# Sums of a head's values in spare columns of the weighted sums' bank

## The chip, the cores and the metric

The kernel runs on one core of a Trainium2 chip. The metric is the time of one execution on the device in microseconds (us); the median of several runs is compared. A core has five engines with a queue of instructions each, which they work off in order: TensorE (PE: matmuls, their weights are loaded by PEld), VectorE (DVE), ScalarE (ACT), GpSimd (POOL) and SyncE (SP, which here issues the DMAs). TensorE writes its results into PSUM, which has eight banks of 512 fp32 columns in each of 128 partitions; VectorE and ScalarE read them there.

## The reference

The program is an attention over clusters followed by two feed-forward layers. 2 batches x 8 heads, 768 tokens, 64 columns a head, 16 centroids a head:

```python
q_assign = argmax(q_n @ c_n.T)           # each query's cluster, k_assign likewise for keys
mask = q_assign[:, :, :, None] == k_assign[:, :, None, :]
scores = where(mask, (q @ k.T) / 8, -1e9)
attn = exp(scores - max(scores)); attn = attn / (sum(attn) + 1e-9)
x = attn @ v                             # heads joined: 1536 x 512
h = x @ moe_w_in;  x = softplus(h) @ moe_w_out
h = x @ moe2_w_in; out = leaky_relu(h, 0.01) @ moe2_w_out
```

A query whose cluster holds no key gets all scores equal, so its result is the mean of all values of the head: for this the sums of a head's values over its 768 keys are needed.

## The kernel before, in words

Fp32 operands are split in two fp16 (or bf16) parts, and a product is built of the products of the parts. The 16 heads run one after another in a software pipeline, with C = 6 tiles of 128 tokens each. For a head h:

- `split` (L288) splits q and k and transposes them by DMA into "t"; `assign_mm` (L300) multiplies them by the centroids: 24 narrow matmuls (L306) into the PSUM bank "as". `assign_el` (L314) makes a one-hot row of each token's cluster in five VectorE steps (L319 to L325), of which the last reads "as". ScalarE writes the one-hot rows behind the 64 columns of q and k ("nq"), and a DMA transposes the whole into "tq" (L331).
- `emit_s1` (L340): masked scores with queries in the partitions (L345), of which VectorE takes maxima "mm" (L352). `emit_m` (L354) brings the maxima into the transposed q ("dg", L359, L361, matmuls L366, copies L374), and marks queries whose cluster is empty.
- `emit_s2` (L377), for a key tile kt of six: scores with keys in the partitions, less the maximum (L392, L393, 384 columns each), exp on ScalarE into "p" (L399), and what bf16 loses of p on GpSimd into "pl" (L401). In heads 0 to 7 the tile kt = 1 goes without "pl": its product is made of fp32.
- `emit_pv` (L406): the weighted sums of the values, six row tiles into the bank "x", 65 columns each (64 and the sum of the weights): L428, L429 and, for pl, L433; in fp32 L415. They take 390 of the 512 columns.
- `emit_sv` (L435): the sums of the head's values, twelve matmuls by a tile of ones (L439, L440) over 65 columns. They are split into a copy "h" (ScalarE, L444) and "svr" (VectorE, L445), both on partitions 96 to 127.
- `emit_empty` (L448): six small matmuls (L451) add these sums to the rows of "x" whose cluster is empty. `emit_norm` (L460) divides (L470, L471, L473) out of "x"; L470 puts six columns behind the 390 to use.

There is one bank "as" and one bank "x" (`PSUM_BUFS`, and the pool px): a new user waits until the last readers of the old one are done. In the program's order "as" is taken by the assignment of head h + 2, then by the sums of head h, then by the assignment of head h + 3. The order of each engine's queue is made when the program is built: a list scheduler takes what it expects to be ready first, by priorities (`at_pri`: the weighted sums of tile j of head h have h + j / 6, the first scores h - 4, the assignment h - 2). The waits between engines are put in where two instructions touch the same tile; for a PSUM tile the whole bank counts.

From head 8 on the first feed-forward layer of the first batch fills TensorE's gaps (`moe_steps`), from head 0 on the weights are read in and split in between (`w_step`, "wcp"). When the attention ends, TensorE runs the feed-forward layers.

Of the kernel before, what the change touches and what calls it, by code (L numbers as in the profile page):

```python
# [43 lines left out]

FF_PRI, FF_STEP, FF_RATE = 8, 0.25, 0.75

W_FREE, W_FROM, W_TO, W_PER = 4, 8, 10, 5
W_PRI = ((0, 0.5), (17, 0.3))
W2_STEPS = 88
# [7 lines left out]
def attn_moe_kernel(  # L57
# [13 lines left out]
    V, S, G, PE = nc.vector, nc.scalar, nc.gpsimd, nc.tensor  # L71
    B, H, SEQ, D = q.shape
    NCL = cen.shape[1]
    DM, DFF = w_in1.shape
    C = SEQ // 128
# [22 lines left out]
    def atile(shape, dt, tag, h):  # L98
        late, early = BUFS[tag]
        n = turn[tag] = turn.get(tag, -1) + 1  # L100
        if h < H and early and n % (late + early) >= late:
            return ep.tile(shape, dt, tag=tag, name=tag, bufs=early)
        return at.tile(shape, dt, tag=tag, name=tag, bufs=late)
# [18 lines left out]
    ones = acon.tile([128, 128], F16, name="ones")  # L122
# [4 lines left out]
    def ring(tag, h=NH):  # L127
        if h < H and tag == "s2":
            n = turn["ps" + tag] = turn.get("ps" + tag, -1) + 1
            if n % (PSUM_BUFS[tag] + 1) == PSUM_BUFS[tag]:  # L130
                return pm.tile([128, 512], F32, tag="m1", name="m")
        return pr.tile([128, 512], F32, tag=tag, name=tag, bufs=PSUM_BUFS[tag])

    mark, tki = {}, {}
    ld_t, tp1, tp2, tpq, p_t, xn_t, as_t, x_t, v_t, svs = ({} for _ in range(10))
# [141 lines left out]
    def load_v(h):  # L277
        b, hh = divmod(h, H)
        vv = v32s[h % V_BUFS][:, :, 0:D]
        nc.sync.dma_start(out=vv, in_=v[b, hh].rearrange("(p c) d -> p c d", c=C))  # L280
        v_t[h] = vv

    def split_v(h):
        vv, v2 = v_t.pop(h), v2s[h % V_BUFS]
        S.copy(out=v2[:, :, D:2 * D], in_=vv)
        ENG[by_group(VLO, h)].tensor_tensor(out=v2[:, :, 0:D], in0=vv, in1=v2[:, :, D:2 * D], op=ALU.subtract)
# [67 lines left out]
    def emit_m(h):  # L354

        dg = dgs[h % len(dgs)]
        diag = dg.rearrange("p (c s) -> p c s", s=129)
        m = diag[:, :, MR:MR + 1]
        mark[h] = V.reduce_max(out=m, in_=mms[h % 2], axis=AX)  # L359
        empty = diag[:, :, MR + C:MR + 3 * C].rearrange("p c (t s) -> p c t s", s=C)[:, :, :, 0]  # L360
        V.tensor_scalar(out=empty, in0=m.to_broadcast([128, C, 2]), scalar1=-65504.0, scalar2=None, op0=ALU.is_equal)  # L361
        t = tp2[h][0]
        for j in range(2):
            bank = ring("s2", h)
            for c in range(3 * j, 3 * j + 3):
                PE.matmul(  # L366
                    out=bank[0:KS2, (c % 3) * 128:(c % 3 + 1) * 128],
                    lhsT=dg[:, c * 128:(c + 1) * 128],
                    rhs=ident,
                    start=True,  # L370
                    stop=True,
                )
            o = bank[MR:KS2, 0:3 * 128].rearrange("p (c r) -> p c r", c=3)
            S.copy(out=t[MR:KS2, 3 * j:3 * j + 3, :], in_=o)  # L374
        tpq[h] = t
# [28 lines left out]
    XW = D + 1  # L404

    def emit_pv(h, kt):  # L406
        v2 = v2s[h % V_BUFS]
        if kt == 0:
            x_t[h] = px.tile([128, 512], F32, tag="x", name="x")
        xps = x_t[h]  # L410
        p, pb, pl = p_t.pop((h, kt))
        if pl is None:
            pf = p.rearrange("p a r -> p (a r)")
            for c in range(C):
                PE.matmul(  # L415
                    out=xps[:, c * XW:(c + 1) * XW],
                    lhsT=pf[:, c * 128:(c + 1) * 128],
                    rhs=v32s[h % V_BUFS][:, kt, :],
                    start=(kt == 0 and c == 0),
                    stop=False,  # L420
                )
            return
        pb = pb.rearrange("p a r -> p (a r)")
        pl = pl.rearrange("p a r -> p (a r)")
        for c in range(C):
            cs = slice(c * 128, (c + 1) * 128)
            o = xps[:, c * XW:(c + 1) * XW]
            PE.matmul(out=o, lhsT=pb[:, cs], rhs=v2[:, kt, D:2 * D + 1], start=(kt == 0 and c == 0), stop=False)  # L428
            PE.matmul(out=o[:, 0:D], lhsT=pb[:, cs], rhs=v2[:, kt, 0:D], start=False, stop=False)  # L429
        for c in range(C):  # L430
            cs = slice(c * 128, (c + 1) * 128)
            o = xps[:, c * XW:(c + 1) * XW]
            PE.matmul(out=o, lhsT=pl[:, cs], rhs=v2[:, kt, D:2 * D + 1], start=False, stop=False)  # L433

    def emit_sv(h):  # L435
        v2 = v2s[h % V_BUFS]
        o = ring("as")[:, 0:XW]
        for kt in range(C):
            PE.matmul(out=o, lhsT=ones, rhs=v2[:, kt, D:2 * D + 1], start=(kt == 0), stop=False)  # L439
            PE.matmul(out=o[:, 0:D], lhsT=ones, rhs=v2[:, kt, 0:D], start=False, stop=(kt == C - 1))  # L440
        q4 = slice(MR, 128)
        h16 = atile([128, XW], F16, "h16", h)
        r = atile([128, XW], F16, "svr", h)
        S.copy(out=h16[q4], in_=o[q4])  # L444
        V.scalar_tensor_tensor(out=r[q4], in0=h16[q4], scalar=sel[q4], in1=o[q4], op0=ALU.mult, op1=ALU.add)  # L445
        svs[h] = r
# [6 lines left out]
    def emit_out(b, hh, xn):  # L453
        nc.sync.dma_start_transpose(
            out=xt[b][:, hh // 2].rearrange("p n (c r) -> p (n c) r", c=C), in_=xn.rearrange("p n c d -> p (n c d)")
        )
# [34 lines left out]
    def open_late():  # L491
        actx.close()
        gp = lctx.enter_context(tc.tile_pool(name="gp", bufs=1))
        late["mt"] = lctx.enter_context(tc.tile_pool(name="mt", bufs=2))
        late["h"] = gp.tile([128, KFF, TB], F16, name="g_h")
        late["l"] = gp.tile([128, KFF, TB], F16, name="g_l")
# [228 lines left out]
    def behind_tk(h):  # L725
        return tc.issue_after(tki[h].ins) if h in tki else nullcontext()

    @contextmanager
    def at_pri(x):
        old = tc.cur_priority  # L730
        tc.cur_priority = pri(x)
        yield
        tc.cur_priority = old
# [8 lines left out]
    with at_pri(-9):  # L742
# [6 lines left out]
            out=ss[:, 1:2], in0=ss[:, 0:1], scalar1=ss[:, 2:3], scalar2=ss[:, 1:2], op0=ALU.mult, op1=ALU.add  # L749
# [19 lines left out]
    for v2 in v2s:  # L769
# [3 lines left out]
        out=ident, in_=ones, pattern=[[1, 128]], compare_op=ALU.is_equal, fill=0.0, base=0, channel_multiplier=-1  # L773
# [4 lines left out]
    for j in range(NCL):  # L778
# [4 lines left out]
        out=sel, in_=sel, pattern=[[0, 1]], compare_op=ALU.is_ge, fill=0.0, base=-MR - 2 * C, channel_multiplier=1  # L783
# [112 lines left out]
    def chain(h):  # L896
        if h < NH:
            with at_pri(h - LEAD_SPLIT):
                split(h)
            with at_pri(h - LEAD_ASSIGN):  # L900
                assign_mm(h)
                assign_el(h)
            with at_pri(h - LEAD_MAX):
                for c in range(C):
                    emit_s1(h, c)
            if h + 2 < NH:
                with at_pri(h - LEAD_LOAD):
                    load(h + 2)

    def moe_steps(n):  # L910
        st["credit"] += n
        while st["credit"] >= 1.0:
            with at_pri(FF_PRI + cnt["m"] * FF_STEP):
                next(ff, None)
            st["credit"] -= 1.0
# [5 lines left out]
    for h in range(NH):  # L921
        with at_pri(h - LEAD_M):
            emit_m(h)
        chain(h + AHEAD)
        wtie["h"] = h + 2
        with at_pri(h):
            if h + 1 < NH:
                split_v(h + 1)
            if h + 2 < NH:
                with behind_tk(h + 2):  # L930
                    load_v(h + 2)
            emit_sv(h)
            if h in outs_t:
                with behind_tk(h + 2):
                    emit_out(*outs_t.pop(h))
        for j in range(C):
            with at_pri(h + j / 6):
                emit_s2(h, j)
                if j:
                    emit_pv(h, j - 1)  # L940
            if h < H - 1 and (j + h * C) % W_PER == 0:
                w_step()
            if h > H or (h == H and j > 0):
                moe_steps(FF_RATE)
            if h == H and j == 0:
                open_late()
        with at_pri(h + 1):
            emit_pv(h, C - 1)
            emit_empty(h)
        with at_pri(h + 1 - LEAD_NORM):  # L950
            emit_norm(h)
# [49 lines left out]
```

## Time and profile before

| | us |
|---|---|
| median of 3 runs | 734.06 (734.0 to 735.52) |
| the profiled execution | 732.15 |
| its span on the core | 730.4 |
| TensorE busy | 677.0 (93%) |
| VectorE busy | 517.3 (71%) |
| ScalarE busy | 410.9 (56%) |
| GpSimd busy | 402.5 (55%) |

The profile lists for every instruction its start, its duration and, where its engine stood still before it, for how long and which other instruction ended that. Ends of matmuls are modelled, since they are pipelined: a matmul of 65 columns is listed with 0.19 us, while the next one starts 0.03 us after it. The attention stage goes from the start to about 314 us, the feed-forward layers beside and behind it to the end.

### The profile page before, as it was taken

How to read it: one execution, taken by the hardware profiler on the slowest of the kernel's cores; microseconds unless marked ns; L12 is line 12 of the kernel's file. 1: busy time of each engine (PE TensorE's matmuls, PEld its weight loads, DVE VectorE, ACT ScalarE, POOL GpSimd, SP SyncE). 2: the span in 40 equal slices, each digit the busy share in tenths (PEclk: the TensorE clock that was granted, in tenths of full speed). 3: DMA queues.
4: the chain of work that ended last, by engine and by line, in shares of the span. 5: the costliest groups of instructions: out<-in, count | busy, mean ns of one | idle time of the engine just before them, and what ended most of it. 6: DMA issues, size and time to landing. Idle time of an engine off the chain costs nothing. (4 is left out here: it accounts for less than half of the span.)

```text
span 730.4 us, 18968 instructions
## 1 busy us (share of the span) xinstructions
PE 677.0 (93%) x7584; PEld 506.7 (69%) x7584; DVE 517.3 (71%) x1167; ACT 410.9 (56%) x1087; POOL 402.5 (55%) x494
## 2 busy tenths in 40 slices
PE   1798899998889899999999999999999999999997
PEld 1367677665656566656666566558999999999996
DVE  4797798998898782069787867965585757575545
ACT  5476666768878753355245425526555555565553
POOL 6387777778888864303324233325556465565653
PEclk9999999999999999999999999999999999999999
DMA  8985966766565632013322355787000000000000
GB/s 204 221 173 113 181 136 122 170 123 173 129 161 152 141 116 53 2 35 103 110 93 82 108 175 193 235 304 261 3 31 2 30 2 7 27 2 31 2 31 30
DMA packets 104521, 77.87 MB, mean 107 GB/s; under 512 B 78320, under 2 KB 92656, under 8 KB 104432
## 3 DMA queue, kind: packets, MB, share of 16 engines
q1 hardware_dynamic: 104288, 76.40, 40.4%
q8 instruction: 59, 0.97, 0.5%
q14 instruction: 30, 0.25, 0.1%
q10 hardware_dynamic: 144, 0.26, 0.1%
HBM read 50.36 MB, written 10.49 MB: 83 GB/s over the span
## 5 line engine op out<-in xcount | busy, mean ns | idle before, releaser
L401 POOL TENSOR_TENSOR pl<-p 128x768 f16<-128x768 f32 x88 | 128.3, 1468 | 56.3 <-ACT p L399 36.0
L352 DVE TENSOR_REDUCE mm<-s 128x1 f32<-128x384 f32 x190 | 100.6, 548 | 19.3 <-PE s L345 16.7
L562 PEld LDWEIGHTS <-w_in2h 128*128 128x128 f16 x1344 | 98.2, 98 | 5.3 <-issue 0.7
L570 DVE TENSOR_TENSOR gl<-r,gh 128x384 f16<-128x384 f32 (+1 forms) x96 | 63.2, 659 | 50.0 <-ACT gh L608 49.3
L697 PE MATMUL m<-xt,w_inh 128*128 128x384 f16 x512 | 93.8, 326 | 4.2 <-ACT rl L521 3.4
L399 ACT ACTIVATE p<-s 128x384 f32<-128x384 f32 x160 | 74.2, 492 | 30.9 <-PE s L393 28.3
L710 PE MATMUL m<-g_l,w_outh 128*128 128x384 f16 x256 | 83.4, 326 | 2.0 <-DVE g_l L511 1.9
L710 PE MATMUL m<-g_h,w_outh 128*128 128x384 f16 x256 | 83.5, 326 | 0.0
L710 PE MATMUL m<-g_h,w_outl 128*128 128x384 f16 x256 | 83.3, 326 | 0.0
L570 POOL TENSOR_TENSOR r<-r,r 128x128 f32<-128x128 f32 x95 | 47.8, 520 | 55.5 <-ACT r L600 55.2
L697 PEld LDWEIGHTS <-w_inh 128*128 128x128 f16 x512 | 49.7, 98 | 38.7 <-issue 6.1
L608 ACT CAST gh<-r 128x384 f16<-128x384 f32 (+1 forms) x96 | 54.2, 565 | 36.6 <-POOL r L570 33.6
L710 PEld LDWEIGHTS <-w_outh 128*128 128x128 f16 x512 | 49.8, 98 | 32.5
L345 PE MATMUL s<-tq 128*128 128x384 f16 x190 | 62.0, 345 | 9.3 <-DMA tq<-nq 4.5
L562 PEld LDWEIGHTS <-gh 128*128 128x128 f16 x672 | 60.5, 98 | 6.4 <-issue 1.1
L200 POOL TENSOR_TENSOR wd<-wd 128x256 f32<-128x256 f32 x32 | 29.3, 925 | 53.9 <-DVE sg L194 39.2
L562 PE MATMUL i<-xt,w_in2h 128*128 128x128 f16 x576 | 57.2, 219 | 0.1
L392 PE MATMUL s<-t 128*128 128x384 f16 x160 | 53.2, 333 | 3.1 <-ACT p L399 2.3
L393 PE MATMUL s<-tq 128*128 128x384 f16 x160 | 53.2, 333 | 1.6 <-ACT tq L374 1.6
L562 PE MATMUL i<-sh,w_in2h 128*128 128x128 f16 x384 | 53.5, 219 | 0.4 <-ACT r L600 0.4
L562 PE MATMUL i<-sl,w_in2h 128*128 128x128 f16 x384 | 53.5, 219 | 0.0
L562 PE MATMUL i<-sh,w_in2l 128*128 128x128 f16 x384 | 53.4, 219 | 0.0
(145 smaller groups left out, 1861.1 us busy)
## 6 DMA issues: line engine op xcount, KB each, us to landing
st<-in_moe_w_in_dram SPq DMA_DIRECT2D x32, 512.0 KB, 4.6
st<-in_moe_w_out_dram SPq DMA_DIRECT2D x32, 512.0 KB, 3.7
kept<-sg SPq DMA_DIRECT2D x16, 256.0 KB, 2.8
qk<-in_q_dram SPq DMA_DIRECT2D x16, 192.0 KB, 3.5
qk<-in_k_dram SPq DMA_DIRECT2D x16, 192.0 KB, 3.7
v<-in_v_dram SPq DMA_DIRECT2D x16, 192.0 KB, 4.7
kept<-sg SPq DMA_DIRECT2D x24, 128.0 KB, 2.7
out_dram<-ob SPq DMA_DIRECT2D x11, 256.0 KB, 2.0
```

Source lines behind the costliest of these rows:

```text
L200: G.tensor_tensor(out=out, in0=in0, in1=in1, op=ALU.subtract)
L345: PE.matmul(out=o, lhsT=t[:, c, :], rhs=tk[:, 3 * j:3 * j + 3, :], start=True, stop=True,)
L352: V.reduce_max(out=mms[h % 2][:, c, j:j + 1], in_=bank[:, 0:3 * 128], axis=AX)
L392: PE.matmul(out=o, lhsT=t1[:, kt, 1, :], rhs=t1[:, 3 * j:3 * j + 3, 0, :], start=True, stop=False)
L393: PE.matmul(out=o, lhsT=t2[:, kt, :], rhs=tqh[:, 3 * j:3 * j + 3, :], start=False, stop=True)
L399: S.activation(out=p[:, j, :], in_=sp, func=AF.Exp, scale=scale)
L401: G.tensor_tensor(out=pl, in0=p, in1=pb, op=ALU.subtract)
L562: one = PE.matmul(out=bank, lhsT=w_, rhs=x_, start=(first and i == 0), stop=(i == len(ops) - 1), skip_group_check=True)
L570: eng.tensor_tensor(out=out, in0=in0, in1=in1, op=op)
L608: S.copy(out=gh[:, lo:hi], in_=r[:, lo:hi])
L697: PE.matmul(out=hp, lhsT=w_, rhs=x_, start=(i == 0), stop=(i == len(ops) - 1))
L710: PE.matmul(out=yp, lhsT=w_[:, kk, ms], rhs=g_[:, kk, :], start=(n == 0), stop=(n == 3 * KFF - 1))
```

## The change

The sums of a head's values are accumulated in columns 396 to 460 of the bank "x" of the same head, not in the bank "as". The first weighted sum of a head starts the bank anew, so the sums start without a start flag of their own. For that `emit_sv(h)` moves: from ahead of the six key tiles of the head to behind the weighted sums of its second tile (kt = 1), which are emitted in step j = 2.

```diff
+SV_AT = 2
 def emit_sv(h):
     v2 = v2s[h % V_BUFS]
-    o = ring("as")[:, 0:XW]
+    o = x_t[h][:, C * XW + C:C * XW + C + XW]
     for kt in range(C):
-        PE.matmul(out=o, lhsT=ones, rhs=v2[:, kt, D:2 * D + 1], start=(kt == 0), stop=False)
-        PE.matmul(out=o[:, 0:D], lhsT=ones, rhs=v2[:, kt, 0:D], start=False, stop=(kt == C - 1))
+        PE.matmul(out=o, lhsT=ones, rhs=v2[:, kt, D:2 * D + 1], start=False, stop=False, skip_group_check=True)
+        PE.matmul(
+            out=o[:, 0:D], lhsT=ones, rhs=v2[:, kt, 0:D], start=False, stop=(kt == C - 1), skip_group_check=True
+        )
...
                 load_v(h + 2)
-        emit_sv(h)
         if h in outs_t:
...
             emit_s2(h, j)
             if j:
                 emit_pv(h, j - 1)
+            if j == SV_AT:
+                emit_sv(h)
```

The line numbers shift by one ahead of the changed function and by three or four behind it: L428 is L429 in the new program, L439 and L440 are L440 and L441, L444 and L445 are L447 and L448.

The scheduler makes a new order of it on all engines. First TensorE at the weighted sums of head 4. Before, the sums of a head stand ahead of the weighted sums of the head before it, and begin with a wait on VectorE, for the reader of "as"; here those of head 5 (v_2_91 are its values), and behind them a score for L352:

```order
1714 L393 MATMUL m<-tq 128x384
1715 L439 LDWEIGHTS ones
1716 L439 MATMUL as<-v_2_91,ones 128x65 [waits DVE_49]
1717 L440 LDWEIGHTS ones
1718 L440 MATMUL as<-v_2_91,ones 128x64
1719 L439 LDWEIGHTS ones
```

Some 60 rows on, the weighted sums of head 4 (values v_1_90) go from pl of kt = 0 over the fp32 product of kt = 1 (L415) straight to kt = 2, without a wait on VectorE:

```order
1781 L433 LDWEIGHTS pl [waits Pool_49]
1782 L433 MATMUL x<-v_1_90,pl 128x65
1783 L415 MATMUL x<-v_1_93,p 128x65 [waits DMAHW3_49]
1784 L415 MATMUL x<-v_1_93,p 128x65 x5
1785 L428 LDWEIGHTS p
1786 L428 MATMUL x<-v_1_90,p 128x65
```

In the new order the twelve sums of head 4 follow the fp32 product; behind the last of them stand two scores for L353 (the old L352), and then the first product of kt = 2, which waits for VectorE:

```order
1856 L440 MATMUL x<-v_1_90,ones 128x65
1857 L346 LDWEIGHTS tq [waits DMAHW3_49]
1858 L346 MATMUL s_1596<-tq 128x384 [waits DVE_49]
1859 L441 LDWEIGHTS ones
1860 L441 MATMUL x<-v_1_90,ones 128x64
1861 L346 LDWEIGHTS tq
1862 L346 MATMUL s_1599<-tq 128x384 [waits DVE_49]
1863 L346 LDWEIGHTS tq
1864 L346 MATMUL s_1602<-tq 128x384 [waits DVE_49]
1865 L429 LDWEIGHTS p
1866 L429 MATMUL x<-v_1_90,p 128x65 [waits DVE_49]
```

The sums have gone from ahead of the burst of weighted sums into it. The same wait stands in all 16 heads; what lies between the last sum and it differs from head to head.

The second place is VectorE at the start, where the maxima of head 0 (mm_95) end. Before, svr of head 0 stands ahead of dg of head 0, and the readers of the fourth assignment (L319 to L323) behind it:

```order
45 L352 TENSOR_REDUCE mm_95<-s_239 128x1 [waits PE_49]
46 L352 TENSOR_REDUCE mm_95<-s_245 128x1 [waits PE_49]
47 L445 SCALAR_TENSOR_TENSOR svr<-h_454,sel,as 32x65 [waits Activation_49,Pool_49]
48 L359 TENSOR_REDUCE dg_102<-mm_95 128x6 [waits DVE_49]
49 L352 TENSOR_REDUCE mm_96<-s_300 128x1 [waits PE_49]
50 L361 TENSOR_SCALAR dg_102<-dg_102 128x6x2 [waits DVE_49]
51 L352 TENSOR_REDUCE mm_96<-s_303 128x1 [waits PE_49]
52 L319 TENSOR_REDUCE mx<-as 128x12 [waits PE_49]
```

Now (line numbers one higher):

```order
45 L353 TENSOR_REDUCE mm_95<-s_239 128x1 [waits PE_49]
46 L320 TENSOR_REDUCE mx<-as 128x12 [waits PE_49]
47 L353 TENSOR_REDUCE mm_95<-s_245 128x1 [waits PE_49]
48 L321 TENSOR_TENSOR as<-as,mx 128x192 [waits DVE_49]
49 L353 TENSOR_REDUCE mm_96<-s_300 128x1 [waits PE_49]
50 L360 TENSOR_REDUCE dg_102<-mm_95 128x6 [waits DVE_49,Pool_49]
51 L322 TENSOR_TENSOR as<-as,tab 128x192 [waits DVE_49]
52 L353 TENSOR_REDUCE mm_96<-s_303 128x1 [waits PE_49]
```

svr of head 0 has left this place (it stands some 25 rows further on), and the fourth assignment's readers have moved ahead by six rows.

## Rows read from the trace of the kernel before

**Rows 1.** The page, busy time, share of the span and instructions:

```profile
PE 677.0 (93%) x7584; PEld 506.7 (69%) x7584; DVE 517.3 (71%) x1167; ACT 410.9 (56%) x1087; POOL 402.5 (55%) x494
```

**Rows 2.** Stretches of the span: us of each, busy time (instructions) of each engine:

```profile
100.00:125.00 25.00, 23.62 (x351) 17.67 (x349) 22.28 (x55) 17.55 (x44) 19.11 (x16) 1.00 0.54 114
...
300.00:400.00 100.00, 99.44 (x675) 60.60 (x673) 71.59 (x134) 46.26 (x99) 29.15 (x18) 1.00 0.24 73
```

**Rows 3.** Waits from 0 to 315 us: who waited for whom, total, times, longest:

```profile
DVE mm L352 <- PE s L345: 16.7, 21, 2.0
...
DVE svr L445 <- ACT h L444: 2.4, 3, 0.8
...
DVE mm L352 <- PE as L439: 1.7, 1, 1.7
...
PE as L439 <- DVE oh L325: 0.8, 2, 0.5
...
PE as L306 <- DVE svr L445: 0.7, 1, 0.7
```

**Rows 4.** Lines of sums and division: count, duration min/median/max ns, first and last start:

```profile
L439 PE MATMUL as<-v,ones x96: 190/193/262, 25.4 to 263.4; 128*128 128x65 f16 x96
...
L444 ACT CAST h<-as x16: 205/210/212, 28.1 to 263.7; 32x65 f16<-32x65 f32 x16
...
L445 DVE SCALAR_TENSOR_TENSOR svr<-h,sel,as x16: 295/296/297, 28.5 to 267.3; 32x65 f16<-32x65 f16 x16
...
L470 DVE TENSOR_SCALAR x<-x x16: 156/163/172, 52.0 to 313.7; 128x6 f32<-128x6 f32 x16
```

**Rows 5.** Timeline, sums of three heads with copy and svr: start, duration, instruction:

```profile
53.30 0.19 PE L440 MATMUL as<-v,ones 128*128 128x64 f16 x1
...
53.53 0.21 ACT L444 CAST h<-as 32x65 f16<-32x65 f32 x1
...
55.01 0.30 DVE L445 SCALAR_TENSOR_TENSOR svr<-h,sel,as 32x65 f16<-32x65 f16 x1
...
81.44 0.19 PE L439 MATMUL as<-v,ones 128*128 128x65 f16 x1
...
81.78 0.19 PE L440 MATMUL as<-v,ones 128*128 128x64 f16 x1
...
84.16 0.21 ACT L444 CAST h<-as 32x65 f16<-32x65 f32 x1
...
84.40 0.30 DVE L445 SCALAR_TENSOR_TENSOR svr<-h,sel,as 32x65 f16<-32x65 f16 x1 [0.84 <-ACT h L444]
...
94.11 0.19 PE L440 MATMUL as<-v,ones 128*128 128x64 f16 x1
...
94.34 0.21 ACT L444 CAST h<-as 32x65 f16<-32x65 f32 x1 [0.23 <-PE as L440]
...
95.17 0.29 DVE L445 SCALAR_TENSOR_TENSOR svr<-h,sel,as 32x65 f16<-32x65 f16 x1
```

**Rows 6.** Timeline, scores (81.8 us) and the bank x over head 4:

```profile
81.80 0.33 PE L392 MATMUL s<-t 128*128 128x384 f16 x1
...
81.97 0.33 PE L393 MATMUL s<-tq 128*128 128x384 f16 x1
...
94.13 0.55 DVE L473 TENSOR_TENSOR y<-x,dd 128x384 f32<-128x384 f32 x1
...
94.80 0.19 PE L428 MATMUL x<-v,p 128*128 128x65 f16 x1
...
100.69 0.19 PE L428 MATMUL x<-v,p 128*128 128x65 f16 x1
...
102.52 0.34 PE L433 MATMUL x<-v,pl 128*128 128x65 f16 x6
...
107.54 0.54 DVE L473 TENSOR_TENSOR y<-x,dd 128x384 f32<-128x384 f32 x1
...
108.13 0.19 PE L428 MATMUL x<-v,p 128*128 128x65 f16 x1
```

## The prediction

> **What bounds the kernel now.** I read the page first, then the table by stage, then who waited for whom in the attention stage, then single heads in order of time. TensorE is busy for 677 of 730.4 us [rows 1], and from 300 us on it has almost no gap: 99.44 of 100 us [rows 2]. What the change touches ends near 314 us, with the division of the last head (L470, last start 313.7) [rows 4], so nothing after that can win or lose by it except through the moment at which attention ends. Before 300 us the picture is different: between 100 and 125 us TensorE (23.62 of 25 us) and VectorE (22.28) are about equally full, GpSimd stands at 19.11 and ScalarE at 17.55 [rows 2]. No engine is at its limit alone; the heads come at the pace at which the engines hand work to each other. The reader is to see that a wait of one microsecond in this stage may cost a microsecond or nothing, depending on whether another engine was late anyway.
>
> **What is removed.** No instruction goes away: the 96 matmuls of L439 and their counterparts of L440, 16 copies (L444, 210 ns) and 16 VectorE operations (L445, 296 ns) stay [rows 4]. What goes is their turn in the one bank "as". In it the sums of a head wait until the assignment of a later head has been read, and the next assignment waits until the sums have been read. In the list of waits that is 0.8 us of TensorE (L439 for the last reader, L325) and 0.7 us (L306 for L445), together 1.5 us [rows 3]. All the other time in which an assignment waits is for its transposed input, or for the assignment ahead of it; that bank stays single, so it stays. I cost the earlier assignments at nothing: the order of VectorE at the start puts one whole assignment ahead by several rows, but its output is a transpose that is used a head later, and what covers it is the row of maxima L352, which waits for TensorE's scores (16.7 us in 21 waits) and not for a transpose [rows 3]. If that cover is thin, the second rival below has its price.
>
> **What is added.** The order of TensorE shows the new wait. The sums now stand behind the weighted sums of the second key tile (kt = 1), in the same bank "x"; the first weighted sum of kt = 2 carries a wait on VectorE that it did not have before, in all 16 heads. It waits until L444 and L445 have read the spare columns, though these are other columns than the ones it writes. Queued behind it on TensorE: the weighted sums of kt = 2 to 5, the next scores for L352, and with them VectorE's maxima.
>
> That this is a wait and no formality is also what the Trainium skill says (PSUM — Partial Sum Buffer, section on bank collisions raising a hardware error): accesses of two engines are to be kept apart by bank and 32-partition quadrant, not by address; disjoint columns do not help. Both readers take partitions 96 to 127 and each weighted sum writes all 128, so by that rule the wait cannot be dropped by the choice of columns; by the naive reading, with disjoint columns free, the added cost would be zero and the sum below would be -1.5 us.
>
> How long is the path through ScalarE and VectorE? The old program ran the same path, where hardly anybody waited for it. From the end of the last sum (start plus duration, modelled) to the end of L445: 53.30 + 0.19 to 55.01 + 0.30 is 1.82 us; 81.78 + 0.19 to 84.70 is 2.73; 94.11 + 0.19 to 95.46 is 1.16 [rows 5]. Mean 1.9 us. The copy sits in ScalarE's queue for up to 2.2 us (81.97 to 84.16), L445 in VectorE's for up to 1.3 us (53.74 to 55.01). With empty queues it would be about 0.04 + 0.24 + 0.30 = 0.6 us (copy 94.34 after 94.30; 84.16 to 84.40; L445 itself).
>
> What covers it is what the order puts between the sums and the waiting product. A score matmul of 384 columns takes 0.17 us from start to start (81.80, 81.97) [rows 6]. The order of the new kernel has there: head 0 eight of them and 24 narrow ones, about 2.0 us; head 1 six, 1.0; heads 2 and 3 eight each, 1.3; head 4 two, 0.3; head 5 six and six narrow, 1.3; head 6 four and six, 1.0; head 7 more than 2; head 8 six, 1.0; head 14 eleven, 1.8; the other heads from 9 on 17 to 24 (the feed-forward's matmuls fill in there), 2.8 and more. With 1.9 us to cover, TensorE stands still for 0.9 (head 1), 0.6, 0.6, 1.6 (head 4), 0.6, 0.9, 0.9 (head 8) and 0.1 us: 6.2 us. With the shortest path seen, 1.16 us, it is 0.2 + 0.9 + 0.2 + 0.2, about 1.4 us; with the longest, 2.73, it is 13.3 us. I take 1.9 because it is the mean of queues as full as the new ones will be.
>
> How much of 6.2 us reaches the end? In head 4 the bank x is taken at 94.80, just after the last reader of the head before (94.13 + 0.55). Its main products end at 100.69 + 0.19, and the last six, on the residuals pl, come only at 102.52 [rows 6]: 1.6 us in which the bank waits for GpSimd. A burst that starts 1.6 us later would still be in time there. And the score matmuls pulled in between are those that GpSimd waits for, so its work moves ahead. I let half of the 6.2 us through: 3.1 us.
>
> **The sum.** -1.5 + 3.1 = +1.6 us. On the profiled execution, 732.15 us (span 730.4 and 1.75 around it), that is 733.75. The profiled execution was 1.9 us below the median of the runs, 734.06; the same +1.6 on the median gives 735.7 us, my forecast.
>
> **Rival one: hidden.** The path is as short as the best one seen and the order covers it: 1.4 us of stalls, half let through, against 1.5 us removed, so -0.8 us, or 733.3; with the small shifts that any new order brings I call it 734, no change. For it: twelve heads have fillers of 1.3 us and more, and the 1.16 us path was read in the busy part. Against it: two of three paths read were longer.
>
> **Rival two: the shared bank set the pace, and the kernel gets faster.** VectorE is nearly as full as TensorE between 100 and 125 us, and two of its waits belong to the sums: 2.4 us (L445 for its copy, three times) and 1.7 us (L352 behind L439) [rows 3]. If VectorE sets the pace and the new order puts other work in front of both, 4.1 us go: 730.0 us. With TensorE's 1.5 us as well it is 728.5. For it: in the old program the sums run right behind the last reader of "as", and the next assignment follows right behind theirs, head after head. Against it: the transposes that come of the assignments are there before they are used, and the copy's wait is moved, not removed.
>
> **Rival three, on the slow side: the bank x sets the pace.** In the trace x is handed on without a gap: the first product of head 4 starts 0.1 us after the last read of head 3 (94.68 to 94.80), that of head 5 0.05 us after head 4's (107.54 + 0.54 to 108.13) [rows 6]. The sums' own 0.5 us (81.44 to 81.97) [rows 5] and the path of 1.9 us now lie inside the time for which a head holds x: 2.4 us more per head. Where pl is late by 1.6 us anyway, 0.8 us remain; where it is not, all 2.4. With 1.5 us in each of heads 1 to 8, 12 us: 746 us. It decides if the last residual products of a head no longer come after a gap. Against it: TensorE has the next head's scores to run meanwhile, and from head 9 on feed-forward matmuls.
>
> **How the numbers follow.** A measurement here cannot tell less than 0.2%, 1.5 us, from no change. Forecast (735.7, some 734.5 to 739) 0.33; hidden 0.25; faster 0.31; slow side 0.11. So faster 0.31, same 0.25, slower 0.44. The likeliest case's own range is 733.5 to 739, which takes in both half and all of the 6.2 us. The range for 8 in 10 takes in rival two down to 728 (both its prices) and reaches up to 743, which is a forecast with the longest path, 13.3 us, let through for two thirds: -1.5 + 8.9 on 734.06 is 741.5, and something for rival three, short of its full price.
>
> **What would show it.** In the changed profile: no sums that wait for a reader of "as", and no assignment that waits for a reader of the sums; a new line in the waits, weighted sums (L428 in the old numbering) that wait for L445, some 6 to 9 times, 0.5 to 1.6 us each and about 6 us in all, the longest in head 4; the copy and L445 1 to 2.7 us behind the last sum; the gap ahead of the last six residual products in heads 1 to 4 shorter than 1.6 us. The attention stage, which ends with the last division near 314 us, should end 1 to 4 us later, and the rest of the program keep its length. I am wrong if that wait is under 2 us in all, if the stage ends earlier although the wait is there (then the bank "as" did hold the heads), or if the difference arises after 315 us.

## The result, and the profile after

The changed kernel takes 741.1 us (738.54 to 744.25, 6 runs), the kernel before 734.03 us in the same series (732.03 to 735.52, 6 runs). The ratio is 1.0102, interval 1.0077 to 1.0127: about 7 us slower. The forecast was 735.7 us, slower by 1.6.

| | before | after |
|---|---|---|
| profiled execution, us | 732.15 | 740.9 |
| its span, us | 730.4 | 739.1 |
| last start of the division, us | 313.7 [rows 4] | 319.6 |
| from there to the end of the span, us (difference) | 416.7 | 419.5 |

So 5.9 us of the 8.7 us of span arise in the attention stage and 2.8 us behind it (two single executions; the medians are 7.1 us apart). In the new program the exponential is L400 and the division starts at L473.

The page of the kernel after, busy time, answers to [rows 1]: TensorE's is the same, VectorE's is 2.0 us more.

```profile
PE 677.0 (92%) x7584; PEld 506.7 (69%) x7584; DVE 519.3 (70%) x1167; ACT 412.0 (56%) x1087; POOL 402.0 (54%) x494
```

Its stretches (columns as in [rows 2]; the third number from the end is the granted clock): the one from 100 us has less work of TensorE (22.74 us for 23.62) and of VectorE (20.42 for 22.28), and a clock of 0.93 for 1.00. The one from 300 us is full.

```profile
100.00:125.00 25.00, 22.74 (x308) 17.69 (x308) 20.42 (x44) 16.58 (x40) 16.70 (x15) 0.93 0.50 114
300.00:400.00 100.00, 100.00 (x718) 61.61 (x716) 66.27 (x126) 43.85 (x95) 26.36 (x17) 1.00 0.22 67
```

Cut at the last division, the two traces can be laid on each other. First the kernel before, 0 to 314 us and the rest:

```profile
0.00:314.00 314.00, 269.67 (x3444) 186.80 (x3444) 229.72 (x533) 203.51 (x493) 215.28 (x202) 0.99 0.62 138
314.00:731.00 417.00, 407.34 (x4142) 319.89 (x4140) 287.55 (x635) 207.44 (x594) 187.26 (x292) 1.00 0.25 83
```

Then the kernel after, 0 to 320 us and the rest:

```profile
0.00:320.00 320.00, 268.92 (x3440) 186.50 (x3441) 232.01 (x533) 204.59 (x493) 215.03 (x202) 0.99 0.59 135
320.00:740.00 420.00, 408.06 (x4146) 320.18 (x4143) 287.27 (x635) 207.41 (x594) 186.93 (x292) 1.00 0.25 82
```

The reader is to see that TensorE has done the same work, some 3440 matmuls, at the end of both stages, with the same busy time to 0.8 us. Nothing was added to its work. It stood still 6.8 us longer (320 - 268.92 against 314 - 269.67).

Within the stage the heads keep level up to the fifth: the last product of head 4 ends at 103.1 us before and at 104.4 after. Four heads later the difference is 9.8 us (160.4 and 170.2). This is that piece, the kernel before:

```profile
103.10:160.40 57.30, 52.64 (x769) 38.35 (x768) 51.78 (x119) 40.27 (x100) 44.38 (x37) 1.00 0.63 133
```

and the kernel after:

```profile
104.40:170.20 65.80, 56.80 (x758) 41.48 (x759) 51.19 (x111) 42.63 (x103) 46.26 (x39) 0.95 0.54 115
```

TensorE idles 9.0 us here instead of 4.7. It is also busy 4.2 us longer for about as many matmuls, at a mean clock of 0.95: from 113.8 to 117.2 us and from 144.5 to 147.9 us the granted clock was 0.50. From head 8 to the end of the stage the new kernel wins 3.9 us back (149.4 us instead of 153.3). That is busy time and no idle time. The kernel before:

```profile
160.40:314.00 153.60, 140.57 (x1608) 93.49 (x1608) 101.53 (x211) 99.57 (x236) 104.58 (x91) 0.99 0.46 114
```

and the kernel after:

```profile
170.20:320.00 149.80, 136.74 (x1605) 91.19 (x1606) 100.53 (x210) 97.24 (x230) 102.54 (x88) 1.00 0.48 117
```

TensorE is idle for 13.0 us in the first and 13.1 in the second. The kernel before has its own stretch at 0.50 here, from 250.7 to 254.1 us.

The waits of the kernel after from 0 to 325 us answer to [rows 3]:

```profile
DVE mm L353 <- PE s L346: 24.1, 36, 2.0
...
PE as L307 <- DMA t<-n: 18.9, 8, 11.6
...
PE s L346 <- DVE mm L353: 7.8, 14, 1.4
...
DVE svr L448 <- ACT h L447: 6.0, 3, 5.2
...
PE x L429 <- DVE svr L448: 2.3, 4, 0.7
PE m L393 <- ACT p L400: 2.3, 1, 2.3
```

The forecast new wait (L429 for L448) is there, 2.3 us in 4 waits. Two others grew more. These are the rows of the kernel before that answer to the second and third, not shown so far:

```profile
PE as L306 <- DMA t<-n: 14.5, 5, 11.7
...
PE s L345 <- DVE mm L352: 4.2, 10, 0.9
```

The assignments wait 4.4 us longer for their transposed input, the score matmuls 3.6 us longer for the maxima. VectorE in turn waits 7.4 us longer for the scores (24.1 against 16.7 [rows 3]). Each engine is late for the other.

The longest single new gap stands in head 5. TensorE's timeline of the kernel after (start, duration, instruction; in brackets the idle time before it and who ended it):

```profile
110.54 0.63 PE L346 MATMUL s<-tq 128*128 128x384 f16 x2
113.43 0.32 PE L393 MATMUL m<-t 128*128 128x384 f16 x1 [2.26 <-ACT p L400]
```

It needs the bank that the exponential (L400) at 112.89 reads. ScalarE's queue shows why that one is late:

```profile
108.83 0.51 ACT L294 CAST nq<-qk 128x384 f16<-128x384 f32 x1 [1.60 <-DMA tq<-nq]
109.25 0.49 ACT L400 ACTIVATE p<-m 128x384 f32<-128x384 f32 x1
...
110.83 0.51 ACT L296 COPY n<-nq 128x384 f16<-128x384 f16 x1
111.23 0.50 ACT L400 ACTIVATE p<-s 128x384 f32<-128x384 f32 x1
111.61 0.52 ACT L296 COPY n<-nq 128x384 f16<-128x384 f16 x1
112.02 0.62 ACT L163 ACTIVATE w_inh<-wcp 128x512 f16<-128x512 f32 x1
112.66 0.21 ACT L447 CAST h<-x 32x65 f16<-32x65 f32 x1
112.89 0.49 ACT L400 ACTIVATE p<-m 128x384 f32<-128x384 f32 x1
```

In this kernel the split of a later head (L294, L296) stands between the exponentials of head 5, waits 1.6 us for a transpose, and holds up what is behind it; a conversion of weights (L163) and the copy of the sums (L447) stand ahead of the last one too. In the kernel before the same split comes behind the last exponential of its burst, where its wait delays none of them:

```profile
109.14 0.48 ACT L399 ACTIVATE p<-m 128x384 f32<-128x384 f32 x1
109.51 0.60 ACT L162 ACTIVATE w_inh<-wcp 128x512 f16<-128x512 f32 x1
112.51 0.92 ACT L293 CAST nq<-qk 128x384 f16<-128x384 f32 x2 [2.40 <-DMA tq<-nq]
```

### The profile page after: what moved, and what is told of

Read it like the earlier page. It is cut to its first block, busy times and chain, and to the rows that moved or that the text cites. A ratio compares the mean times of both kernels' runs of the same rounds, so it can differ in the third digit from the quotient of the medians.

```text
span 739.1 us, 18971 instructions
## 1 busy us (share of the span) xinstructions
PE 677.0 (92%) x7584; PEld 506.7 (69%) x7584; DVE 519.3 (70%) x1167; ACT 412.0 (56%) x1087; POOL 402.0 (54%) x494
## 4 chain that ended last, share of the span: by engine, by line
PE 67%; DVE 12%; DMA 11%; ACT 4%; issue 3%; POOL 2%; SPq 1%; DVEq 0%; ACTq 0%; POOLq 0%
PE m L713 14%; PE i L565 14%; PE acc L565 14%; PE m L700 12%; DMA t<-n 5%; DVE mm L353 2%; PE s L393 2%; PE s L346 2%; PE s L394 2%; DMA tq<-nq 2%; DMA st<-in_moe_w_in_dram 1%; DMA v<-in_v_dram 1%; PE x L429 1%; PE x L434 1%; PE x L430 1%
## 5 line engine op out<-in xcount | busy, mean ns | idle before, releaser
L353 DVE TENSOR_REDUCE mm<-s 128x1 f32<-128x384 f32 x190 | 100.7, 549 | 24.6 <-PE s L346 24.1
L573 DVE TENSOR_TENSOR gl<-r,gh 128x384 f16<-128x384 f32 (+1 forms) x96 | 63.8, 665 | 49.8 <-ACT gh L611 49.1
L400 ACT ACTIVATE p<-s 128x384 f32<-128x384 f32 x160 | 74.3, 491 | 29.1 <-PE s L394 25.3
L713 PE MATMUL m<-g_l,w_outh 128*128 128x384 f16 x256 | 83.4, 326 | 4.5 <-DVE g_l L514 4.5
L713 PE MATMUL m<-g_h,w_outh 128*128 128x384 f16 x256 | 83.5, 326 | 0.3 <-ACT rl L524 0.2
L713 PE MATMUL m<-g_h,w_outl 128*128 128x384 f16 x256 | 83.3, 326 | 0.0
L713 PEld LDWEIGHTS <-w_outh 128*128 128x128 f16 x512 | 49.8, 98 | 33.6 <-issue 0.8
```

The costliest lines, as they stand in the source:

```text
L353: V.reduce_max(out=mms[h % 2][:, c, j:j + 1], in_=bank[:, 0:3 * 128], axis=AX)
L400: S.activation(out=p[:, j, :], in_=sp, func=AF.Exp, scale=scale)
L573: eng.tensor_tensor(out=out, in0=in0, in1=in1, op=op)
L713: PE.matmul(out=yp, lhsT=w_[:, kk, ms], rhs=g_[:, kk, :], start=(n == 0), stop=(n == 3 * KFF - 1))
```

## The experiments

Four theories were on record in turn. A: the new wait inside the bursts costs the 7 us. B: the sums' turn in the bank of the assignment had held the assignments to the pace of the heads; freed, they run ahead. C: any other order of the queues costs some us. D: the sums, hidden before in idle time of TensorE, now stand in the bursts of heads 4 to 8. The scheduler orders all queues anew for each of these kernels, so each comes with its own order. Ratios are to the kernel before in the same runs. Its median was between 734.03 and 735.36 us from series to series, so kernels of different series are better compared by their ratios than by their medians.

| kernel | median us | ratio, interval | profiled span us | TensorE waits before 330 us | us at clock 0.50, 45 to 330 us |
|---|---|---|---|---|---|
| before | 734.03 | 1 | 730.4 | 43.3 | 3.4 |
| e12_before_split2 | 732.63 | 0.9968, 0.9952 to 0.9983 | 732.2 | 43.4 | 10.2 |
| e10_before_w45 | 737.87 | 1.0034, 1.0005 to 1.0063 | 738.0 | 47.7 | 10.2 |
| e14_after_split2 | 737.95 | 1.0041, 1.0024 to 1.0058 | 734.8 | 47.4 | 6.8 |
| e8_x_late | 738.02 | 1.0042, 1.0011 to 1.0074 | 736.9 | 47.7 | 6.8 |
| e3_tied | 739.05 | 1.0056, 1.0036 to 1.0076 | 737.4 | 46.1 | 6.8 |
| e7_nosums | 740.1 | 1.0056, 1.0023 to 1.0089 | 741.0 | 50.6 | 13.7 |
| e4_noread | 740.84 | 1.0093, 1.0059 to 1.0128 | 736.3 | 47.3 | 6.8 |
| after | 741.1 | 1.0102, 1.0077 to 1.0127 | 739.1 | 49.6 | 6.8 |
| e9_x_early | 741.99 | 1.0084, 1.0055 to 1.0114 | 737.4 | 49.8 | 3.4 |
| e2_x_at5 | 742.54 | 1.0102, 1.0063 to 1.0140 | 740.7 | 49.2 | 10.2 |
| e13_x_hold | 743.92 | 1.0115, 1.0089 to 1.0142 | 742.3 | 50.4 | 13.7 |
| e5_tied_noread | 745.54 | 1.0156, 1.0098 to 1.0213 | 741.9 | 52.0 | 10.2 |
| e11_before_sixth | 748.5 | 1.0182, 1.0138 to 1.0225 | 749.3 | 53.7 | 34.1 |

The fifth column is the sum of all rows of TensorE in the list of waits from 0 to 330 us. The sixth is worked out from the clock records of each trace. It begins at 45 us since the record of some executions begins late: that of the kernel before reads 1.00 from the start, but its score matmuls start 0.32 us apart up to 39.0 us and 0.16 us apart behind that.

```profile
38.20 0.53 PE L392 MATMUL s<-t 128*128 128x384 f16 x1
38.52 0.53 PE L393 MATMUL s<-tq 128*128 128x384 f16 x1
...
39.27 0.33 PE L393 MATMUL m<-tq 128*128 128x384 f16 x1
39.43 0.33 PE L392 MATMUL s<-t 128*128 128x384 f16 x1
```

**e2_x_at5**: the sums three key tiles later in the burst.

```
-SV_AT = 2
+SV_AT = 5
```

> The changed kernel with SV_AT = 5: the sums stand behind the weighted sums of the fifth key tile (kt = 4), just ahead of the last. Only the products of kt = 5 wait for svr, and these wait for GpSimd's pl anyway. Theory A: 736 to 738, since most of the path lies beside the wait for pl. Theory B: 740 to 742, as the assignments are as far ahead as in the changed kernel. Theory C: anywhere from 733 to 742.

Measured 742.54 us; TensorE waits for svr in all 3.1 us. No gain from another place of the sums in the burst.

**e3_tied**: the assignment's matmuls of head h come on TensorE only after the maxima's products of head h-3, about where they stood before.

```
-                assign_mm(h)
+                with tc.issue_after(mpe[h - 3].ins) if h - 3 in mpe else nullcontext():
+                    assign_mm(h)
```

> The changed kernel, with one order put back: the 24 assignment matmuls of head h may not be issued on TensorE before the matmuls that bring in the maxima of head h - 3 (the place they had before the change). The sums stay in the bank x and the wait of the weighted sums for svr stays. Changed kernel 741.1 us, before 734.0. Theory A (the wait inside the burst of weighted sums costs the 7 us): 740 to 742, waits of assignments for their transposes may shrink and nothing comes of it. Theory B (the freed bank lets the scheduler put assignments up to 35 us of work ahead in TensorE's queue, where they wait for transposes, 18.9 us against 14.5): 734 to 736. Theory C (any new order of the queues moves the time by some us): anywhere from 733 to 742.

Measured 739.05 us, 2 us under the kernel after by the medians and 3 by the ratios, but still 4 us above before by its ratio. Its waits for transposed input fell from 18.9 to 13.9 us, and waits for the exponentials rose from 3.4 to 8.7: the gap moved.

**e4_noread**: copy and svr read a small tile of zeros, so that no weighted sum waits for them (the mean for empty clusters is left out).

```
-        S.copy(out=h16[q4], in_=o[q4])
+        S.copy(out=h16[q4], in_=sz[q4])
```

(and the same in svr)

> The changed kernel without the read of the bank x between its weighted sums: the copy and svr take a constant tile of zeros in SBUF, so the sums are computed and not used (the mean for queries with an empty cluster is left out). Same instructions on every engine; no weighted sum waits for svr. The assignments stay ahead in TensorE's queue. Theory A: 734 to 736, since the wait and the copy in ScalarE's queue cannot hold the bank any more. Theory B: 740 to 742. Theory C: anywhere from 733 to 742.

Measured 740.84 us with no wait for svr left. Theory A asked for the kernel before's time, and falls in this form: without the wait the loss is still there (0.9%), though in another order.

**e5_tied_noread**: both edits.

> Both edits together: assignments tied to their old place on TensorE, and copy and svr fed with zeros in place of the sums (the mean for queries with an empty cluster is left out). Theory A: as e4, 734 to 736. Theory B: as e3, 734 to 736. If both A and B hold with about half each, e3 and e4 stand near 737.5 and this one at 734 or just below. Theory C: no pattern between the three.

Measured 745.54 us, 5 us more than e4 and 6 more than e3. The parts don't add up, which is the first sign that the order is measured along with the part.

**e7_nosums**: the 192 matmuls of the sums left out; copy and svr from zeros.

> The kernel after without the 192 matmuls of the sums; copy and svr take zeros from a small tile instead (the mean that empty clusters get is left out). Nothing of the sums is left on TensorE, and the assignments run ahead as in the kernel after. By the kernel after's rows the 192 matmuls are 18.4 us of its TensorE time. Theory D (the sums' place: what the kernel before hid in idle TensorE time ahead of the bursts now stands in the bursts of heads 4 to 8): most of the 18.4 us was hidden before, so this kernel comes out only 0 to 6 us under the kernel before (728 to 734 us) and 7 to 13 us under the kernel after. Theory B (the assignments run ahead, whatever the sums do): this kernel keeps what the kernel after lost, and is no faster than the kernel before (734 to 740 us). If the sums cost their whole time in both kernels: 716 to 722 us.

Measured 740.1 us: leaving out the 192 matmuls gained 1 us on the kernel after by the medians and 3 by the ratios, and it is still 4 us slower than the kernel before, which does that work. Theory D in this form falls. But the 18.4 us of the expectation are no such saving. They add up two lines whose modelled durations overlap. Taken together, the 192 matmuls of the kernel after cover 10.2 us (first number behind the length):

```profile
0.00:330.00 330.00, 10.20 (x192) 8.38 (x192) 0.60 (x3) 0.99 0.58 132
```

Where twelve stand together they take 0.36 us from start to start (81.44 to 81.80 [rows 5, rows 6]), so 16 heads have some 6 us of them, an estimate. And TensorE's busy time did not fall: its page shows 2.0 us more than that of the kernel after, with 13.7 us at the lower clock in place of 6.8.

```profile
PE 679.0 (92%) x7392; PEld 502.1 (68%) x7392; DVE 524.8 (71%) x1167; ACT 412.5 (56%) x1087; POOL 402.8 (54%) x495
```

So the run speaks against a stage that goes at the pace of TensorE's work, but its own order and the clock are not separated from the work left out.

**e8_x_late** and **e9_x_early**: the sums of one half of the heads in each bank.

```
+SV_X = lambda h, H: h >= H       (e9: h < H)
+        o = x_t[h][:, ...] if SV_X(h, H) else ring("as")[:, 0:XW]
```

> Sums of heads 0 to 7 in the bank of the assignment as before, those of heads 8 to 15 in the bank of the weighted sums as after. TensorE's order is word for word the kernel before's up to the bursts of head 7. Theory D (the loss arises in heads 5 to 8, where the kernel after's heads end 9 us late; behind them it gains back 3.4 us): head 8 ends at 163 us as before, the attention stage ends 0 to 3 us earlier, 729 to 734 us. Theory C (any other order of the queues than the one of the kernel before costs some us): 737 to 745 us.

> The other half: sums of heads 0 to 7 in the bank of the weighted sums as after, those of heads 8 to 15 in the bank of the assignment as before. TensorE's order is word for word the kernel after's up to the bursts of head 7. Theory D: the loss of heads 5 to 8 is there (head 8 ends at 170 to 173 us) and is not gained back, 740 to 745 us. Theory C: 737 to 745 us as well, but then the twin with the halves exchanged is as slow.

Measured 738.02 and 741.99 us. With TensorE's order of before up to head 7, that head's products end at 142.2 us (142.6 before): the early loss is gone. (The 163 us that the expectation has for head 8 of the kernel before are 160.4 by its trace.) But this kernel loses 5.8 us by the end of the stage, where the kernel after had won some back. Its twin has the early loss again, and at the very same instruction, behind the same row of ScalarE's queue (line numbers one higher again):

```profile
116.40 0.32 PE L394 MATMUL m<-t 128*128 128x384 f16 x1 [2.42 <-ACT p L401]
```

So the early loss belongs to that order and repeats with it. D's forecast for e8, a gain, failed.

**e10_before_w45**, a control: the kernel before with one priority of the weight conversions changed.

```
-W_PRI = ((0, 0.5), (17, 0.3))
+W_PRI = ((0, 0.45), (17, 0.3))
```

> The kernel before with one number of the order of its weight conversions changed (0.5 to 0.45): the sums stay in the bank of the assignment; TensorE's order changes only from about 160 us on. It is a control for how much a mere change of order moves the time. Theory C: 737 to 745 us. Theories B and D: no part of them is touched, 732 to 736 us.

Measured 737.87 us: 2.5 us lost with no bank moved, by an order that differs only from about 160 us on. The interval of its ratio begins at 1.0005, so the loss is just clear of noise.

**e11_before_sixth**: the kernel before with two of the twelve matmuls of the sums.

```
-        for kt in range(C):
+        for kt in range(1):
```

> The kernel before with a sixth of the sums: two matmuls in place of twelve (one of six tiles of values; the mean for empty clusters is not the whole one), copy and svr as before. The bank of the assignment is taken between two assignments as before, so that the assignment of head 8 stands at 54 us of TensorE work in its order (57 in the kernel before, 39 in the kernel after, 37 in the one without sums). Theory B (the sums' turn in that bank holds the assignments to the pace of the heads; freed, they run ahead and everything behind them is late): as fast as the kernel before, 732 to 736 us, and 4 to 8 us under the kernel without any sums, though that one does less. Theory C (any other order than the one of the kernel before costs some us): 737 to 742 us.

Measured 748.5 us, the slowest of all, with the bank taken as before and less work. Theory B's 732 to 736 is out, and C's 742 is exceeded too. It also spent 34.1 us at the lower clock, ten times as long as the kernel before.

**e12_before_split2**, a second control.

```
-LEAD_SPLIT, ... = 2.5, ...
+LEAD_SPLIT, ... = 2, ...
```

> A second control: the kernel before with the priority of the splits of queries and keys lowered (2.5 to 2 heads ahead). The sums and their bank are as before, the assignments stand where they stood (head 8 at 58 us of TensorE work), but ScalarE's order changes from its 18th instruction on, in a quarter of its places. Theory C: 737 to 745 us, with no bank moved at all. Theory B: 732 to 736 us.

Measured 732.63 us, 0.3% faster than the kernel before and so than both kernels. C in the form "every other order costs" falls: a new order can win. Its heads reach 314 us in another way (head 8's products end at 166.3 us, 5.9 later than before, and the last head's at 314.2), so a late head 8 alone does not make a late end. TensorE's busy time at the end of the stage is the same:

```profile
0.00:315.00 315.00, 270.04 (x3438) 185.69 (x3439) 230.37 (x533) 205.50 (x493) 214.64 (x202) 0.98 0.61 137
```

**e13_x_hold**: the kernel after, with a stand-in (one matmul, a copy, a VectorE operation) that takes the old bank where the sums did.

```
+        o = ring("as")[:, 0:XW]
+        PE.matmul(out=o, lhsT=ones, rhs=v2s[...][:, 0, D:2 * D + 1], start=True, stop=True)
+        S.copy(out=hold[q4, 0], in_=o[q4])
+        V.scalar_tensor_tensor(out=hold[q4, 1], in0=hold[q4, 0], scalar=sel[q4], in1=o[q4], ...)
```

> The kernel after (the sums, copy and svr in the bank of the weighted sums), and beside it a stand-in that takes the bank of the assignment where the kernel before did: one matmul, a copy and a VectorE operation of the same sizes, whose result nobody reads (16 times 0.2 us of ScalarE and 0.3 us of VectorE more). The assignment of head 8 comes at 51 us of TensorE work. Theory B: the kernel before's time comes back, 733 to 737 us. Theory C: 737 to 745 us. Were it the sums' place inside the bursts: 739 to 744 us.

Measured 743.92 us. With the turn put back the time did not come back. Theory B falls as the whole cause.

**e14_after_split2**: the kernel after with the priority of e12.

> The kernel after with the priority of the splits lowered as in the control that gained with the sums in the bank of the assignment (2.5 to 2 heads ahead). The sums stay in the bank of the weighted sums and the assignments stay early (head 8 at 39 us of TensorE work). If the new bank costs its 7 us whatever the order, and the priority its gain of 2.4 us likewise: 738 to 740 us. If the loss belongs to the one order that the scheduler drew for the kernel after: it can come out anywhere between 731 and 748 us, the span of the re-ordered kernels so far, and its time will follow TensorE's waits before 330 us (44 us of them go with 733 to 735, 48 with 738, 50 with 741 to 743, 54 with 748).

Measured 737.95 us, 3.1 us under the kernel after by the medians and 4.5 by the ratios, at 47.4 us of waits as that column had it. The bank and the early assignments are as in the kernel after. TensorE never stands still for svr in it, and it waits longer than any of the others for the transposed input, though it is faster than the kernel after:

```profile
PE as L307 <- DMA t<-n: 23.1, 9, 11.8
```

So a part of the loss goes with the order. But the same priority gained 2.4 us in the old bank too (e12). Under it the move of the sums costs 1.0041 / 0.9968 = 1.0073, about 5 us, and under the old priority 1.0102, about 7 us. The difference of these two is within their intervals. The first alternative of the expectation, 7 us for the bank less 2.4 for the priority (738 to 740), is all but met.

**What the runs say together.** The time goes with the sum of TensorE's waits in the attention stage: over the 14 profiles the span rises by about 1.5 us for each us of it, with a correlation of 0.93 (worked out from the table). This describes the loss and is not by itself its cause. The time at the lower clock goes along with it (sixth column), and the two were not separated. No one wait carries it. From before to after it is the transposed input (14.5 to 18.9 us) and the maxima; in e3 the exponentials; in e11 the division that hands x on, which is TensorE's second largest wait there:

```profile
PE as L306 <- DMA t<-n: 17.6, 5, 12.6
PE x L428 <- DVE y L473: 5.6, 5, 2.2
```

Shown, then: TensorE's new wait is no more than 2.3 us of the loss where it stands, and the loss is there without it (e4, e14); the freed turn put back did not bring the time back (e13); orders with no bank moved differ by 5 us (732.6 to 737.9), and those with the sums whole in x and read by 6 (738.0 to 743.9). Since each edit came with an order of its own, e4, e7 and e13 speak against their theories as the whole cause, and do not price the parts.

Open: how much of the 7 us the move of the sums costs on the mean over orders, and by what. The three kernels with whole sums in the old bank stand at -0.3, 0 and +0.3%; the five with whole sums, read, in the new one (after, e2, e3, e13, e14) at +0.4 to +1.2%. The two groups don't overlap, though the intervals of e10 and e14 do, and the move costs time under both priorities (e12 and e14). That speaks for a cost of its own beside that of the order; with so few orders its size is not shown. Two kernels in one and the same order that differ in the bank alone were not tried.

## Why the prediction was right in its sign and wrong in its size

- **What bounds the stage**: right as far as the runs show. At the end of both stages TensorE's busy time is the same to 0.8 us and the difference is idle time; with 192 matmuls less (e7) the kernel is still slower than the kernel before.
- **What is removed**: the two waits (0.8 and 0.7 us) are gone from the trace as forecast. The assignments' other waits were said to stay; they grew by 4.4 us.
- **"I cost the earlier assignments at nothing"**: this step failed; how much of the loss it is stays open. The cover named was L352, which waits for scores and not for transposes. That was true of the old order. It did not ask what else is reordered when a bank comes free: in the kernel after, the split of a later head stands among the exponentials of head 5, and TensorE stands still for 2.26 us. The rest of that step, "the small shifts that any new order brings", was a phrase in place of a term. The controls put that term at -2.4 us (e12) to +2.5 us (e10) without any edit to the sums: more than the whole sum that was forecast (+1.6).
- **What is added**: the mechanism was right, the term mis-sized. Forecast were 6 to 9 waits, 6.2 us, the longest in head 4. Measured were 4 waits, 2.3 us: 0.60 us in head 1, 0.69 in head 4 (the longest), 0.61 in head 8, 0.40 in head 13 (where none was forecast). The mean path in heads 0 to 8, from the sums' last end to svr's end, is 1.94 us (1.9 forecast). So the mean path was right; putting the mean into every head was the error. In heads 2, 3 and 6, where a wait was forecast and none came, the path took only 1.10, 0.77 and 0.85 us. In head 4 it took 1.64 us and the cover was 0.95, not 0.3; 0.35 of it were waits of TensorE for the maxima, which the forecast did not count as cover. In head 5, where the path took 4.0 us, TensorE was held by the exponential instead. With the longest path the terms add up to 13.6 us, not 13.3; nothing hangs on it. By the Trainium skill (PSUM — Partial Sum Buffer, section on bank collisions raising a hardware error), which goes by bank and quadrant and not by address, the wait is due in spite of disjoint columns. The program sets it, and the trace shows what it cost, these four waits; no run here shows what would come without it.
- **"Half of it reaches the end"**: cannot be read. e4 lost the wait and not the time, but its order is another too.
- **The sum**: +1.6 us forecast, about +7 measured. It was right in sign, but not for its reason: of 8.7 us of span, the wait that it was built on is 2.3 at most. That 741.1 lies within the range up to 743 is luck as well: that end was built on the longest path in every head, 13.3 us of waits.
- **"The rest keeps its length"**: wrong by 2.8 us in this profile. Behind the stage the second feed-forward product waits 4.5 us for its input (L713, page of after); it was 1.9 before:

```profile
L713 PE MATMUL m<-g_l,w_outh 128*128 128x384 f16 x256 | 83.4, 326 | 4.5 <-DVE g_l L514 4.5
```

- **The three signs of a wrong prediction**: none was met as written, two nearly. The wait is 2.3 us, not under 2, and a third of the difference arises after 315 us. Of the other forecasts, the stage ends 5.9 us later, not 1 to 4. The gap ahead of the last six residual products is under 1.6 us in heads 3 and 4 (1.08 and 0.32 us), but not in heads 1 and 2 (2.30 and 2.42).
- **The rivals**: one (hidden) is out by the time, though the waits came nearer to its 1.4 us than to 6.2. Two (faster) is out for this order. Three (x sets the pace) named heads 1 to 8, and the loss is in heads 5 to 8; but the last residual products still come after a gap in heads 1 to 8 (0.32 to 2.92 us), and e7 has neither sums nor a wait for svr in x and loses as well. That speaks against the path inside x as the whole cause.

## What to carry to other kernels

Where a scheduler orders the queues, an edit that frees a buffer orders the whole program anew, and the new order is a cost of its own. Measure its size first with one or two neutral changes (a priority), and don't give a cause to a difference that these reach. Then measure the edit under each of these orders: here the move cost about 7 us in one and about 5 in the other, which one pair of kernels could not have told. In a stage that runs at the pace at which engines hand work to each other, neither a removed wait of 2 us nor 192 removed matmuls need show in the time. And add up overlapping durations as one stretch before calling them a saving.

## What the runs showed of the hardware that was not expected

Behind the gap in head 5 the granted clock of the kernel after fell to its lower level, 1.2 GHz (0.50), for some 3 us: TensorE was busy 0.74 of 3 us in 111 to 114, and all of the time after it.

```profile
111.00:114.00 3.00, 0.74 (x6) 0.42 (x5) 1.80 (x5) 2.33 (x6) 3.00 (x4) 0.97 0.85 245
114.00:117.00 3.00, 3.00 (x45) 2.66 (x43) 2.67 (x6) 0.85 (x2) 1.00 (x1) 0.50 0.07 24
117.00:120.00 3.00, 3.00 (x46) 2.22 (x44) 2.22 (x5) 2.09 (x5) 1.18 (x1) 0.96 0.00 0
```

In e9, behind a gap of 2.42 us at the same instruction (113.98 to 116.40, so it begins ahead of the first stretch), it stayed at 1.00:

```profile
115.00:118.00 3.00, 1.60 (x31) 1.28 (x31) 2.27 (x6) 2.15 (x6) 2.94 (x3) 1.00 0.60 172
118.00:121.00 3.00, 3.00 (x61) 2.35 (x58) 3.00 (x6) 1.50 (x4) 0.65 (x1) 1.00 0.00 0
```

So a gap of about this length at this instruction was followed by the lower level in one execution and not in the other. The two kernels with the least matmul work, e7 and e11, spent 13.7 and 34.1 us of the stage at the lower level, the kernel before 3.4. In e11 the clock is at its lower level for whole stretches in which TensorE is full:

```profile
117.00:120.00 3.00, 3.00 (x24) 2.83 (x24) 1.44 (x4) 2.71 (x7) 3.00 (x4) 0.50 0.41 111
120.00:123.00 3.00, 3.00 (x48) 2.66 (x46) 2.44 (x8) 0.45 (x2) 0.97 (x1) 0.50 0.78 231
156.00:159.00 3.00, 3.00 (x11) 1.34 (x10) 2.65 (x8) 2.59 (x7) 3.00 (x4) 0.50 0.42 130
```

That less work ran longer was the surprise of this case. With score matmuls 0.32 us apart at one level and 0.16 at the other, 34.1 us at the lower one are up to 17 us lost, an estimate, and 1.7 us in the kernel before. That would be up to 15 of the 18.9 us by which the profiled execution of e11 is longer, and by the same working up to 5 of the 10.6 us of e7. It is not shown as a cause: six of the seven falls in e11 came behind a gap of TensorE of 0.85 us or more, and the gaps come with the order.
